# Decode attention over a 4096-key window: one value group's load cut in halves, the output rows ahead of the last values, 360 instead of 320 rows on five DMA engines

## The chip, the core and the metric

One core of a Trainium2 chip. The core has five engines with their own instruction queues: TensorE (PE in the profile, PEld for its weight loads), VectorE (DVE), ScalarE (ACT), GpSimd (POOL) and SyncE (SP), and 16 DMA engines, which carry the transfers that SP and ACT issue. Matmul results go to PSUM, everything else lies in SBUF, on 128 partitions. The metric is the device time of one execution, in microseconds. The kernel before took 194.53 us in the median of 8 runs (194.44 to 195.16).

## The reference, cut to what matters

There is one token, x of 512 elements. Two branches start from its layer norm xn, and the output is `x + s * g`:

```python
q = (xn @ wq) as 32 heads of 128
k, v = the last W = 4096 rows of k_cache, v_cache, per head
scores = q . k * 128 ** -0.5
o = softmax(scores) @ v
s = o (4096 elements) @ wo            # wo: 4096 x 512

g = silu(xn + hs + gelu(layernorm(xn + hs) @ w3) @ w4)    # w3: 512 x 1376, w4: 1376 x 512
```

`hs` is a small shifted product with `w2`. All tensors are bf16. Keys and values of one head are 1 MB each, so 64 MB of the cache are read, beside 4 MB each of `wq` and `wo` and some 3 MB of the other weights.

## The kernel before, in words

The 32 heads are worked on in eight groups of four (`G = 4`). A group's keys are one tile of 128 partitions x 128 rows x 128 elements: each head has 32 partitions, and each partition 128 successive positions, 32 KB in one piece. The values lie the same way. One load is 4 MB.

The loop at the end of the kernel goes over `s = 0 ... 9`. Step `s` scores group `s` and multiplies the values of group `h = s - 2` (`LAG = 2`). The scores of a group are split over two ways: the first 64 or 80 of the 128 rows by VectorE (`k_vector`, L301 and L303), the rest on TensorE (`k_turn`, `k_scores`, with copies on ScalarE, L319). `sm_...` is the softmax. `v_part` (L423) multiplies 128 value tiles into `oT`, one matmul each; `v_out` scales with the reciprocal of the sum (L442 for the last two groups). Three tiles for keys (`K_BUFS`) and two for values (`V_BUFS`) are used in turn, so a load waits until the tile's last reader is done.

All loads but x's are issued by SP, in the order of the code (`load`). Eight semaphores tell of landings and are given to the transfers in turn; a transfer whose semaphore is still in use by an earlier one waits on SP until that one has landed. The order of TensorE, VectorE and ScalarE in the loop is that of the code (`manual_schedule`).

The output product is done in three blocks of heads: 0 to 15 (`y_wide`), 16 to 23 (`y_block(1)`), and 24 to 31, the block `few_block`. For this last one, `wo` lies in two forms. The first `FEW = 320` rows are in `wo_few`, loaded by `load_few`: each of its two transfers has an outermost dimension of `NE = 5`, and each piece of it is four runs of 8 KB; so these rows come by the lowest five DMA engines. To use rows in this layout, `ox_few` spreads the attention output by a matmul with a 0/1 matrix `few` and gives `of`; `y_block(few_block)` multiplies. The rows after that are in `wo_rows`, a head each (`load_rows`, `y_head`): 64 rows of head 26 (`r_part = 64`; `h_part = 26`), then heads 27 to 31. Each output matmul (L150) is four of 128 columns, onto four partitions of `y_ps`.

The end of the kernel, which the change touches: at `s = 7`, SP issues the values of group 5, the rows of block 1 and `load_few`. At `s = 8` it issues the values of group 6 in one load, at `s = 9` the rows of heads 26 and 27, the values of group 7 in three pieces (`cuts = (0, 64, 112, 128)`), and the rows of heads 28 and 29, of 30 and of 31. At `s = 8`, TensorE multiplies block 1 and then group 6's values; VectorE makes `of`. At `s = 9` TensorE takes the first 64 value tiles of group 7, then `wo_few`'s block and the rows of heads 26 and 27, then the other value tiles, then heads 28 to 31. VectorE multiplies the sum with `g` (L602), adds x (L604), and SP stores.

`w4` (1376 rows) is loaded in three transfers, of 8 x 128, 2 x 128 and 96 rows; the columns of `w3` are taken in the order that goes with it (`chunks`).

Of the kernel before, what the change touches and what calls it, by code (L numbers as in the profile page):

```python
# [8 lines left out]
P = 128  # L9
BF16 = mybir.dt.bfloat16  # L10
FP32 = mybir.dt.float32
# [10 lines left out]
NE = 5  # L22
# [7 lines left out]
def kernel(  # L30
# [16 lines left out]
    Bb, Sq, D = A_x.shape  # L47
# [7 lines left out]
    CP = G * W // P  # L55
    PB = P // G
    KC = D // P
    F = B_w3.shape[1]
    assert F == 8 * P + 2 * P + 96
    scale = float(Dh) ** -0.5  # L60


# [3 lines left out]
    const = ctx.enter_context(tc.tile_pool(name="const", bufs=1))  # L66
    small = ctx.enter_context(tc.tile_pool(name="small", bufs=1))
    ps_misc = ctx.enter_context(tc.tile_pool(name="ps_misc", bufs=1, space=PSUM))
# [2 lines left out]
    ps_o = ctx.enter_context(tc.tile_pool(name="ps_o", bufs=1, space=PSUM))  # L71
    ps_y = ctx.enter_context(tc.tile_pool(name="ps_y", bufs=1, space=PSUM))
    sm_pool = ctx.enter_context(tc.tile_pool(name="sm", bufs=3))
    small.tile([P, 112], BF16, name="pad")
    wts_guard = tc.tile_pool(name="wts", bufs=1)
    wts = wts_guard.__enter__()

    def load(dst, src):
        return tc.keep_in_program_order(nc.sync.dma_start(out=dst, in_=src))
# [8 lines left out]
    w3_sb = wts.tile([P, KC, F], BF16, name="w3_sb")  # L88
    load(w3_sb[:], B_w3.rearrange("(p c) n -> p c n", p=P))
    w4_sb = wts.tile([P, 11, D], BF16, name="w4_sb")  # L90
    load(w4_sb[:, 0:8, :], B_w4[0:8 * P, :].rearrange("(p c) n -> p c n", p=P))
    load(w4_sb[:, 8:10, :], B_w4[8 * P:10 * P, :].rearrange("(p c) n -> p c n", p=P))
    load(w4_sb[0:96, 10, :], B_w4[10 * P:F, :])
    wq_sb = wts.tile([P, KC, HD], BF16, name="wq_sb")
    load(wq_sb[:], A_wq.rearrange("(p c) n -> p c n", p=P))
# [1 line left out]
    def load_kv(pool, cache, g, cuts=(0, CP)):  # L97
        t = pool.tile([P, CP, Dh], BF16, tag="kv", name="kv")
        src = cache[0, G * g:G * g + G, W0:, :].rearrange("a (b c) d -> b a (c d)", b=PB)
        dst = t[:].rearrange("p c d -> p (c d)")  # L100
        for c0, c1 in zip(cuts, cuts[1:]):
            load(dst[:, c0 * Dh:c1 * Dh], src[:, :, c0 * Dh:c1 * Dh])
        return t

    ident_bf = const.tile([P, P], BF16, name="ident_bf")
# [95 lines left out]
    nc.vector.tensor_scalar(out=xn_row[:], in0=x_row[:], scalar1=negmean[:], scalar2=rstd[:],  # L201
                            op0=ALU.add, op1=ALU.mult)

    chunks = [(P, slice(r, 8 * P, 8)) for r in range(8)]
    chunks += [(P, slice(8 * P + r, 10 * P, 2)) for r in range(2)]
    chunks += [(96, slice(10 * P, F, 1))]
    a_ps = ps_misc.tile([P, 11], FP32, tag="misc", name="a_ps")
    for j, (m, cols) in enumerate(chunks):
# [45 lines left out]

    few = const.tile([P, 2, 32], BF16, name="few")
    nc.vector.memset(few[:], 0.0)
    for c in range(2):
        nc.vector.tensor_copy(  # L260
            out=few[:, c, 0:4 * NE].rearrange("p (a b) -> p a b", b=4),
            in_=ident_bf[:, 4 * NE * c:4 * NE * (c + 1)].rearrange("p (b a) -> p a b", b=4))

# [112 lines left out]
    blocks = [(0, 16), (16, 8), (24, 8)]  # L378
    few_block = 2
    few_h = blocks[few_block][0]  # L380
    FEW = 8 * 8 * NE
    h_part = few_h + FEW // P

    r_part = FEW % P
    o_blk, wo_blk, ox_blk = {}, {}, {}

    def load_wo(i):
        h0, n = blocks[i]
        load(wo_blk[i], A_wo[h0 * P:(h0 + n) * P, :].rearrange("(p t) n -> p t n", p=P))

    def load_few():
        t = wo_blk[few_block]
        for c in range(2):
            r0 = few_h * P + c * FEW // 2
            load(t[32 * c:32 * c + 4 * NE],
                 A_wo[r0:r0 + FEW // 2, :].rearrange("(b a t) n -> a b (t n)", b=4, a=NE))

    def wo_row(h):
        return wo_rows[:, h - h_part, :]
# [1 line left out]
    def load_rows(h, n):  # L401
        if h == h_part:
            load(wo_rows[r_part:P, 0, :], A_wo[h * P + r_part:(h + 1) * P, :])
            h, n = h + 1, n - 1
        load(wo_rows[:, h - h_part:h - h_part + n, :],
             A_wo[h * P:(h + n) * P, :].rearrange("(h p) n -> p h n", p=P))
# [3 lines left out]
    def v_part(g, v, c0=0, c1=CP):  # L410
        s = st[g]
        if g in MOVED:
            s["ov"] = ps_o.tile([4 * G, 4, Dh], FP32, tag="oT", name="ov")
            for c in range(0, CP, 4):
                nc.tensor.matmul(s["ov"][:], lhsT=s["pT"][:, c:c + 4, :].rearrange("p i a -> p (i a)"),  # L415
                                 rhs=v[:, c:c + 4, :], start=(c == 0), stop=(c == CP - 4))
            s["ov_sb"] = sm_pool.tile([4 * G, 4, Dh], FP32, tag="ov_sb", bufs=1, name="ov_sb")
            nc.scalar.copy(out=s["ov_sb"][:], in_=s["ov"][:])  # L418
            return
        if c0 == 0:  # L420
            s["oT"] = ps_o.tile([P, G], FP32, tag="oT", name="oT")
        for c in range(c0, c1):
            nc.tensor.matmul(s["oT"][:], lhsT=v[:, c, :], rhs=s["pT"][:, c, :], start=(c == 0),  # L423
                             stop=(c == CP - 1))
# [44 lines left out]
        ox_blk[i] = ox  # L469

    def ox_few(i):
        of_ps = ps_misc.tile([64, 8], FP32, tag="misc", name="of_ps")
        nc.tensor.matmul(of_ps[:], lhsT=few[:].rearrange("p a b -> p (a b)"), rhs=ox_blk[i][:],
                         start=True, stop=True)
        of = sm_pool.tile([64, 8], BF16, tag="of", bufs=1, name="of")
        nc.vector.tensor_copy(out=of[:], in_=of_ps[:])
        ox_blk[i] = of

# [22 lines left out]
    NG = H // G  # L501
    cuts = (0, 64, 112, CP)
# [3 lines left out]
    v_pool = None  # L506
    for s in range(NG + LAG):
        h = s - LAG
        last = h == NG - 1
        kn = load_kv(k_pool, A_k_cache, s, (0, 64, CP) if s == 0 else (0, CP)) if s < NG else None  # L510
        if s == LAG:
            wts_guard.__exit__(None, None, None)
            v_pool = ctx.enter_context(tc.tile_pool(name="v", bufs=V_BUFS))
            wo_blk[few_block] = v_pool.tile([64, 8, D], BF16, tag="wo_few", bufs=1, name="wo_few")
            nc.gpsimd.memset(wo_blk[few_block][:], 0.0)
            wo_rows = v_pool.tile([P, H - h_part, D], BF16, tag="wo_rows", bufs=1, name="wo_rows")
            nc.gpsimd.memset(wo_rows[0:r_part, 0, :], 0.0)
        if last:
            load_rows(h_part, 2)
            v = load_kv(v_pool, A_v_cache, h, cuts)  # L520
            for r, n in ((H - G, 2), (H - 2, 1), (H - 1, 1)):
                load_rows(r, n)
        elif h >= 0:
            v = load_kv(v_pool, A_v_cache, h)
        if h == 3:
            wo_24 = k_pool.tile([P, 32, D], BF16, tag="kv", name="wo_24")
            wo_blk[0], wo_blk[1] = wo_24[:, 0:16, :], wo_24[:, 16:24, :]
            load_wo(0)
        if h == 5:
            load_wo(1)  # L530
            load_few()

        if s < NG:
            nb = len(batches(s))

            def keys(b0, b1):
                for b in range(b0, b1):
                    k_turn(s, kn, b)
                    if b > 0:
                        k_scores(s, b - 1)  # L540

            k_open(s)
            k_vector(s, kn, 0)
            keys(0, 2)
            if s > 1:
                sm_den(s - 2)
                sm_rden(s - 2)
            if h - 1 in MOVED:
                v_add(h - 1)
                v_out(h - 1)  # L550
            keys(2, 4)
            k_vector(s, kn, 1)
            if s > 0:
                sm_turn(s - 1)
            if s == 6:
                ox_spread(0)
            keys(4, nb)
            k_scores(s, nb - 1)
            sm_own(s)
            if s > 0:  # L560
                sm_exp(s - 1)
            k_vector(s, kn, 2)
            if s == 6:
                ox_pick(0)
            k_vector(s, kn, 3)
            if h >= 0:
                v_part(h, v)
            sm_max(s)
            if s == 6:
                y_wide(0, 0, 16)  # L570
            if h >= 0 and h not in MOVED:
                v_out(h)
        elif s == NG:

            sm_den(NG - 2)
            sm_rden(NG - 2)
            sm_turn(NG - 1)
            ox_spread(1)
            sm_exp(NG - 1)
            ox_pick(1)  # L580
            y_block(1)
            rows_add(y_ps, one_f, y_row, False)
            v_part(h, v)
            v_out(h)
            ox_spread(few_block)
            sm_den(NG - 1)
            sm_rden(NG - 1)
            ox_pick(few_block)
            ox_few(few_block)
        else:  # L590
            v_part(h, v, 0, cuts[1])
            y_block(few_block)
            for r in range(h_part, H - G):
                y_head(r)
            for c0, c1 in zip(cuts[1:], cuts[2:]):
                v_part(h, v, c0, c1)
            v_out(h)
            for r in range(H - G, H):
                y_head(r)
# [36 lines left out]
```

## Time and profile before

| What | Value |
|---|---|
| median of 8 runs | 194.53 us (194.44 to 195.16) |
| the profiled execution | 194.47 us, of which the span is 192.7 us |
| bytes read from memory | 78.84 MB, 409 GB/s over the span |
| busy, share of the span | PE 69%, PEld 52%, DVE 76%, ACT 44%, POOL 3% |
| the chain that ended last | DVE 51%, DMA 23%, PE 15%, ACT 4%, issue 4% |
| instruction fetches in the span | queue q8: 16 packets, 0.26 MB; q14: 3 packets, 0.02 MB |
| mean granted TensorE clock | 0.696 of full speed |

The span runs from the first to the last instruction. The chain that ended last is followed back from the last instruction, at each step to what released it. "DMA" as a share is the mean busy share of the 16 DMA engines. A line such as L423 is one of the kernel's source, and in a group or a timeline row the columns are the start, the duration, engine, line, operation, `out<-in`, the shapes and the count. Time to landing is from the issue of a transfer to its completion semaphore.

### The profile page before, as it was taken

How to read it: one execution, taken by the hardware profiler on the slowest of the kernel's cores; microseconds unless marked ns; L12 is line 12 of the kernel's file. 1: busy time of each engine (PE TensorE's matmuls, PEld its weight loads, DVE VectorE, ACT ScalarE, POOL GpSimd, SP SyncE). 2: the span in 40 equal slices, each digit the busy share in tenths (PEclk: the TensorE clock that was granted, in tenths of full speed). 3: DMA queues.
4: the chain of work that ended last, by engine and by line, in shares of the span. 5: the costliest groups of instructions: out<-in, count | busy, mean ns of one | idle time of the engine just before them, and what ended most of it. 6: DMA issues, size and time to landing. Idle time of an engine off the chain costs nothing.

```text
span 192.7 us, 4716 instructions
## 1 busy us (share of the span) xinstructions
PE 132.2 (69%) x2098; PEld 99.5 (52%) x2098; DVE 145.8 (76%) x160; ACT 85.6 (44%) x193; POOL 6.5 (3%) x14
## 2 busy tenths in 40 slices
PE   0549774967625579878586994981888878843882
PEld 0444364756524433467475343881768256832771
DVE  1550207999999999999999999996899999950201
ACT  2003003888895270458357413771475069841000
POOL 2110007000000000000000000000000000000000
PEclk9999955596975556985558699555555599855555
DMA  6999999999999999999999999999999999999980
GB/s 203 412 488 422 398 429 459 417 435 412 422 432 435 435 437 432 435 435 429 432 432 435 435 432 401 469 432 415 435 432 437 418 435 393 447 416 393 423 332 15
DMA packets 4869, 79.13 MB, mean 411 GB/s; under 512 B 682, under 2 KB 1482, under 8 KB 1866
## 3 DMA queue, kind: packets, MB, share of 16 engines
q1 hardware_dynamic: 4698, 78.84, 96.1%
q8 instruction: 16, 0.26, 0.6%
q10 hardware_dynamic: 152, 0.00, 0.0%
q14 instruction: 3, 0.02, 0.0%
HBM read 78.84 MB, written 0.00 MB: 409 GB/s over the span
## 4 chain that ended last, share of the span: by engine, by line
DVE 51%; DMA 23%; PE 15%; ACT 4%; issue 4%; POOL 1%; SPq 0%; ACTq 0%; POOLq 0%
DVE S L303 30%; DVE prod L301 16%; DMA kv<-in_A_k_cache_dram 13%; DMA kv<-in_A_v_cache_dram 9%; ACT kt L319 3%; PE yr_ps L489 3%; PE oT L423 3%; PE hr_ps L221 2%; DMA x_bf<-in_A_x_dram 2%; PE qT_ps L237 2%; PE a_ps L210 1%; PE hr_ps L218 1%; DVE S L339 1%; DVE m L341 1%; PE sT L325 1%
## 5 line engine op out<-in xcount | busy, mean ns | idle before, releaser
L303 DVE TENSOR_REDUCE S<-prod 128x20 f32<-128x2560 bf16 (+1 forms) x32 | 83.8, 2620 | 1.1
L319 ACT COPY kt<-pt 128x1024 bf16<-128x1024 bf16 x54 | 52.9, 1014 | 23.9 <-PE pt L317 23.2
L317 PE MATMUL pt<-ident_bf,kv 128*128 128x128 bf16 x432 | 43.7, 267 | 10.0 <-DMA kv<-in_A_k_cache_dram 7.2
L301 DVE TENSOR_TENSOR prod<-kv,q_bc 128x2560 bf16<-128x2560 bf16 (+1 forms) x32 | 44.3, 1386 | 5.3 <-DMA kv<-in_A_k_cache_dram 2.5
L317 PEld LDWEIGHTS <-kv 128*128 128x128 bf16 x432 | 35.1, 122 | 12.4 <-DMA kv<-in_A_k_cache_dram 7.5
L325 PE MATMUL sT<-qT_bf,kt 128*128 128x4 bf16 x432 | 20.0, 168 | 17.3 <-ACT kt L319 16.5
L325 PEld LDWEIGHTS <-kt 128*128 128x128 bf16 x432 | 16.6, 104 | 24.7 <-ACT kt L319 24.5
L423 PE MATMUL oT<-pT,kv 128*128 128x4 bf16 x768 | 21.5, 166 | 3.5 <-DMA kv<-in_A_v_cache_dram 3.4
L423 PEld LDWEIGHTS <-kv 128*128 128x128 bf16 x768 | 21.0, 103 | 5.3 <-DMA kv<-in_A_v_cache_dram 5.2
L415 PE MATMUL ov<-kv,pT 128*16 128x512 bf16 x64 | 18.6, 463 | 0.0
L363 ACT ACTIVATE pT<-S,mb 128x128 bf16<-128x128 f32 x32 | 13.9, 569 | 0.3
L415 PEld LDWEIGHTS <-pT 128*16 128x16 bf16 x64 | 6.5, 105 | 11.1 <-issue 6.4
L442 DVE TENSOR_TENSOR o<-oT,rden 128x4 bf16<-128x4 f32 x2 | 0.3, 162 | 13.5 <-PE oT L423 13.5
L334 ACT ACTIVATE own<-sT,par 128x48 f32<-128x48 f32 (+1 forms) x32 | 7.6, 359 | 3.7 <-PE sT L325 3.7
L363 ACT ACTIVATION_READ_ACCUMULATOR pT<-S,mb 128x1 f32 x32 | 8.1, 254 | 0.0
L446 ACT ACTIVATE o<-oT,rden 128x1 bf16<-128x1 f32 x24 | 4.3, 260 | 8.5 <-PE oT L430 5.0
L418 ACT COPY ov_sb<-ov 16x512 f32<-16x512 f32 x2 | 1.2, 576 | 14.6 <-PE ov L415 14.6
L224 DVE COPY hr<-hr_ps 1x512 f32<-1x512 f32 x1 | 0.7, 679 | 8.9 <-PE hr_ps L221 8.9
L347 PE MATMUL mt_ps<-ident_f,m 128*1 128x128 f32 x8 | 2.9, 359 | 5.0 <-DVE rden L374 5.0
L489 PE MATMUL yr_ps<-wo,ox 128*1 128x512 bf16 x16 | 5.4, 513 | 0.9 <-DVE ox L467 0.9
L213 ACT ACTIVATE a_bf<-a_ps 128x10 bf16<-128x10 f32 x1 | 0.2, 180 | 12.0 <-PE a_ps L210 12.0
L356 PE MATMUL mb_ps<-md,par_t 5*128 5x4 f32 x16 | 3.9, 314 | 2.3 <-DVE md L351 1.5
(113 smaller groups left out, 90.8 us busy)
## 6 DMA issues: line engine op xcount, KB each, us to landing
kv<-in_A_k_cache_dram SPq DMA_DIRECT2D x7, 4096.0 KB, 31.1
kv<-in_A_v_cache_dram SPq DMA_DIRECT2D x7, 4096.0 KB, 30.5
wq_sb<-in_A_wq_dram SPq DMA_DIRECT2D x1, 4096.0 KB, 17.8
kv<-in_A_k_cache_dram SPq DMA_DIRECT2D x2, 2048.0 KB, 21.3
wo<-in_A_wo_dram SPq DMA_DIRECT2D x1, 2048.0 KB, 30.1
kv<-in_A_v_cache_dram SPq DMA_DIRECT2D x1, 2048.0 KB, 13.8
kv<-in_A_v_cache_dram SPq DMA_DIRECT2D x1, 1536.0 KB, 16.8
w_sb<-in_B_w_dram SPq DMA_DIRECT2D x1, 1376.0 KB, 6.8
```

The source lines that it names most:

```text
L301: nc.vector.tensor_tensor(out=prod[:, 0:m, :], in0=kn[:, rows, :], in1=q_bc[:, g:g + 1, :].to_broadcast([P, m, Dh]), op=ALU.mult)
L303: nc.vector.tensor_reduce(out=st[g]["S"][:, rows], in_=prod[:, 0:m, :], axis=AX.X, op=ALU.add)
L317: nc.tensor.transpose(pt[:, c - c0, :], kn[:, c, :], ident_bf[:])
L319: nc.scalar.copy(out=kts[b][:, 0:c1 - c0, :], in_=pt[:, 0:c1 - c0, :])
L325: nc.tensor.matmul(st[g]["sT"][:, c - nd(g), :], lhsT=kt[:, c - c0, :], rhs=qT_bf[:, G * g:G * g + G], start=True, stop=True)
L334: nc.scalar.mul(s["own"][:, 0:m, a], s["sT"][:, 0:m, a], par[:, a:a + 1])
L356: nc.tensor.matmul(mb_ps[:], lhsT=par_t[:].rearrange("k b a -> k (b a)"), rhs=md[:], start=True, stop=True)
L363: nc.scalar.activation(out=s["pT"][:, :, a], in_=s["S"][:], func=ACT.Exp, scale=scale, bias=mb[:, a:a + 1], accum_out=s["sum"][:, a:a + 1])
L415: nc.tensor.matmul(s["ov"][:], lhsT=s["pT"][:, c:c + 4, :].rearrange("p i a -> p (i a)"), rhs=v[:, c:c + 4, :], start=(c == 0), stop=(c == ...
L423: nc.tensor.matmul(s["oT"][:], lhsT=v[:, c, :], rhs=s["pT"][:, c, :], start=(c == 0), stop=(c == CP - 1))
L446: nc.scalar.mul(o_blk[b][:, c + k:c + k + 1], st[g]["oT"][:, k:k + 1], st[g]["rden"][:, k:k + 1])
L489: nc.tensor.matmul(yr[i][:], lhsT=ox_blk[i][:, t:t + 1], rhs=wo_blk[i][:, t, :], start=(t == 0), stop=(t == n - 1))
```

## The change

- The values of group 6, the last but one, are loaded in two halves of 64 rows, each with its own semaphore.
- At `s = 9`, TensorE does `wo_few`'s block and heads 26 and 27 first, and then all value tiles of group 7.
- `FEW` is 360 instead of 320: `wo_few` is loaded in three transfers of 5 x 3 runs of 8 KB, and 24 instead of 64 rows of head 26 are left for `wo_rows`. The 0/1 matrix and its result become 96 wide.
- `w4`'s first 1280 rows come in one load instead of two, with ten rows per partition, and the columns of `w3` follow it.
- A pad of 112 elements becomes one of 80.

```diff
-    small.tile([P, 112], BF16, name="pad")
+    small.tile([P, 80], BF16, name="pad")
...
-    load(w4_sb[:, 0:8, :], B_w4[0:8 * P, :].rearrange("(p c) n -> p c n", p=P))
-    load(w4_sb[:, 8:10, :], B_w4[8 * P:10 * P, :].rearrange("(p c) n -> p c n", p=P))
+    load(w4_sb[:, 0:10, :], B_w4[0:10 * P, :].rearrange("(p c) n -> p c n", p=P))
...
-    chunks = [(P, slice(r, 8 * P, 8)) for r in range(8)]
-    chunks += [(P, slice(8 * P + r, 10 * P, 2)) for r in range(2)]
+    chunks = [(P, slice(r, 10 * P, 10)) for r in range(10)]
...
-    few = const.tile([P, 2, 32], BF16, name="few")
+    few = const.tile([P, 3, 32], BF16, name="few")
     nc.vector.memset(few[:], 0.0)
-    for c in range(2):
+    for c in range(3):
         nc.vector.tensor_copy(
-            out=few[:, c, 0:4 * NE].rearrange("p (a b) -> p a b", b=4),
-            in_=ident_bf[:, 4 * NE * c:4 * NE * (c + 1)].rearrange("p (b a) -> p a b", b=4))
+            out=few[:, c, 0:3 * NE].rearrange("p (a b) -> p a b", b=3),
+            in_=ident_bf[:, 3 * NE * c:3 * NE * (c + 1)].rearrange("p (b a) -> p a b", b=3))
...
-    FEW = 8 * 8 * NE
+    FEW = 9 * 8 * NE
...
-        for c in range(2):
-            r0 = few_h * P + c * FEW // 2
-            load(t[32 * c:32 * c + 4 * NE],
-                 A_wo[r0:r0 + FEW // 2, :].rearrange("(b a t) n -> a b (t n)", b=4, a=NE))
+        for c in range(3):
+            r0 = few_h * P + c * FEW // 3
+            load(t[32 * c:32 * c + 3 * NE],
+                 A_wo[r0:r0 + FEW // 3, :].rearrange("(b a t) n -> a b (t n)", b=3, a=NE))
...
-        of_ps = ps_misc.tile([64, 8], FP32, tag="misc", name="of_ps")
+        of_ps = ps_misc.tile([96, 8], FP32, tag="misc", name="of_ps")
...
-        of = sm_pool.tile([64, 8], BF16, tag="of", bufs=1, name="of")
+        of = sm_pool.tile([96, 8], BF16, tag="of", bufs=1, name="of")
...
-            wo_blk[few_block] = v_pool.tile([64, 8, D], BF16, tag="wo_few", bufs=1, name="wo_few")
+            wo_blk[few_block] = v_pool.tile([96, 8, D], BF16, tag="wo_few", bufs=1, name="wo_few")
...
-            v = load_kv(v_pool, A_v_cache, h)
+            v = load_kv(v_pool, A_v_cache, h, (0, 64, CP) if h == NG - 2 else (0, CP))
...
         else:
-            v_part(h, v, 0, cuts[1])
             y_block(few_block)
             for r in range(h_part, H - G):
                 y_head(r)
-            for c0, c1 in zip(cuts[1:], cuts[2:]):
+            for c0, c1 in zip(cuts, cuts[1:]):
                 v_part(h, v, c0, c1)
```

More of the change, by code (lines that the diff above doesn't have):

```diff
@@ L58 @@
     F = B_w3.shape[1]
-    assert F == 8 * P + 2 * P + 96
+    assert F == 10 * P + 96
     scale = float(Dh) ** -0.5
```

## The prediction

> **What bounds the kernel now.** I read the DMA part of the page first, then the chain that ended last, the TensorE timeline of the end, and the DMA share over the last microseconds.
>
> The row of DMA busy tenths over 40 slices, and the queues:
>
> ```profile
> DMA  6999999999999999999999999999999999999980
> q1 hardware_dynamic: 4698, 78.84, 96.1%
> q8 instruction: 16, 0.26, 0.6%
> q14 instruction: 3, 0.02, 0.0%
> ```
>
> The 16 DMA engines are full from the second slice to the last but one: the span is the time of 78.84 MB. VectorE's large shares of the chain lie in the middle, where it runs beside full DMA engines. So the end is looked at, first in the chain of waits (start, us, what):
>
> ```profile
> 169.65 16.80 DMA kv<-in_A_v_cache_dram
> ...
> 186.50 1.88 PE oT L423 x64
> ...
> 188.62 0.71 PE y_ps L150 x16
> ```
>
> and in the TensorE timeline (start, us, instructions, in brackets the idle time before and who ended it):
>
> ```profile
> 177.52 3.57 PE L423 MATMUL oT<-pT,kv 128*128 128x4 bf16 x128 [2.92 <-DMA kv<-in_A_v_cache_dram]
> ...
> 182.86 1.87 PE L423 MATMUL oT<-pT,kv 128*128 128x4 bf16 x64
> 184.66 1.02 PE L150 MATMUL y_ps<-wo_few,of 64*1 64x128 bf16 x32
> 185.61 0.38 PE L150 MATMUL y_ps<-wo_rows,o 128*1 128x128 bf16 x8
> 186.50 1.87 PE L423 MATMUL oT<-pT,kv 128*128 128x4 bf16 x64 [0.51 <-DMA kv<-in_A_v_cache_dram]
> ```
>
> TensorE waits for a transfer at 177.5 (all of group 6's values) and at 186.5 (the second piece of group 7's). The last transfer of all, the rows of head 31, was issued at 177.5; the tile view of `wo_rows`, cut to that issue, gives its time to landing:
>
> ```profile
> DMA to landing us min/median/max: 11.5/11.5/11.5
> ```
>
> It lands at 189.0, and the last four matmuls start at 189.03, after a short gap: values and last rows end together, and both are transfers. Last, the windows (length, then busy time of each engine, granted clock, DMA share, GB/s):
>
> ```profile
> 182.00:185.00 3.00, 2.31 (x82) 2.19 (x85) 0.65 (x3) 0.00 (x0) 0.00 (x0) 0.50 0.97 398
> 185.00:187.00 2.00, 1.49 (x54) 0.99 (x43) 0.00 (x0) 0.00 (x0) 0.00 (x0) 0.50 0.83 322
> 187.00:189.00 2.00, 1.75 (x64) 1.58 (x62) 0.16 (x1) 0.00 (x0) 0.00 (x0) 0.50 0.39 138
> ```
>
> The share falls over 4 us: the engines end unevenly, and the slowest ends the kernel. Which one that is, the packet records tell. They hold start, duration, size and queue of each packet; an engine starts a packet some 4 ns before its previous one ends, so the packets join into 16 chains, and the five that carry 8 KB packets of `wo_few` are the five low engines. My joining (us from the span's start; v5 is value group 5, and so on):
>
> ```
> engines            v5 ends        few ends   v6 ends        v7 piece 2     last packet
> A, B, C            160.8-161.0    165.7-.9   175.4-175.5    184.6-184.8    187.2-187.4
> D                  161.8          166.7      176.5          185.6          188.3
> E                  162.2          167.1      176.95         186.04         188.67
> three without few  160.9-161.2    -          173.0-173.4    182.3-182.7    184.9-185.3
> eight without few  162.4-164.3    -          174.7-176.6    184.1-185.8    186.7-188.4
> ```
>
> E, one of the five, is last at every mark. It is late because it fetched 8 KB of instructions twice (at 70.0 and 147.0): eight 32 KB packets take an engine 9.68 us, 10.36 with such a fetch, 11.2 with one of 16 KB, of which the lower eight rows of the table have two each.
>
> **The change part by part.**
>
> *360 rows.* Each of the five engines carried 2 x 4 packets of 8 KB, now 3 x 3. A packet takes 309 ns, less 4 of overlap, and each transfer ends in a 9 ns semaphore packet: +0.305 + 0.009 = +0.314 us. The rows left of head 26 fall from 64 (four 1 KB packets per engine) to 24. A 1 KB packet takes 46 ns, 42 net. How 24 rows are split no row shows: between two per engine and all on one (24 x 0.042 = 1.0 us, +0.84 over now, if that one is E). 64 rows spread evenly on 16 and 20 pieces evenly on five, so I take two each: -0.084 on E. [...]
>
> *Group 6 in halves.* Sixteen 16 KB packets for eight of 32 KB: 16 x (611 - 4) = 9712 ns against 8 x (1213 - 4) = 9672, and one more semaphore: +0.045. The semaphore packet is 9 ns within a stream that is full. [...]
>
> *w4 in one load.* Eight packets of 8 KB and eight of 2 KB (84 ns) become eight of 10 KB, estimated at 385 ns, halfway between 309 (8 KB) and 460 (12 KB): 3048 against 3080 ns, and a semaphore less: -0.037.
>
> *TensorE's order.* Half of group 6's 128 matmuls can run before 177.5: its first half should land near 172.6 (half of 9.7 us earlier), and TensorE is free from 174.6. So oT ends some 1.7 us earlier, near 179.5, the chain to `of` (181.1 to 183.0 now) near 181.3, and the 32 + 8 output matmuls (1.02 + 0.38) fill the wait before the first piece of group 7, which lands at 182.8. Its 64 matmuls then end near 184.9 where TensorE was done at 186.0. None of it shortens the path: the next thing is the second piece, at 186.45, and TensorE already had 0.51 us of idle time there. A gain is excluded while that transfer is last; a loss starts only if the new order is over 1.9 us late (186.7 - 184.8).
>
> *Issues and waits.* SP issues one load fewer at the start, one more of few (0.83 us) and one more for group 6 (0.58), all far ahead: group 6's values are issued at 149.4 and reached at 163.4 at the earliest. Eight completion semaphores are taken in turn, so the shift of one changes what SP waits for: the 24 rows now wait for keys 7, head 27's rows for values 5, the last two rows for the halves of group 6. Behind them on SP stands group 7's first piece, issued at 169.05 when TensorE has freed its buffer; values 5 must have landed before that matmul (165.6), so nothing is later. If it landed after 169.05, group 7 would be. The last rows' issue still follows group 6's landing (177.5), 7 us before any engine reaches it.
>
> *Small tiles.* `few` has a third 128x15 copy on VectorE in the prologue, POOL fills 96 partitions where it filled 64 (3.5 us at 30.0, the load at 132): covered by full DMA queues, and by the 13 us between the issue of keys 6 at 111.5 and 124.4, when the queue reaches them. The pad moves addresses only.
>
> The sum on E: 0.314 - 0.084 + 0.045 - 0.037 = +0.24 us, for both its second piece (186.04) and its last packet (188.67), hence for the end. The next engine's last packet (188.37) gets no few rows and doesn't overtake. The profiled execution took 194.47 us (span 192.7 and 1.8 around it), 0.06 under the median 194.53. Its end moves to 194.71; against the median, 194.77.
>
> **The rivals.**
>
> *The five engines are relieved (faster).* E's lateness is two fetches of 0.68 us and D's is one (about 1.0). If the changed program's fetches fall on other engines, D and E end near 187.6, and the others set the end at 188.37 - 0.08: 0.4 us earlier, 194.1. For it: the placing depends on the program. Against: instruction counts are almost equal, and the same engine was hit twice.
>
> *One more fetch on a late engine (slower).* It decides as soon as one more 8 KB fetch falls on E, or a 16 KB one on any that ends after 187.4: 0.24 + 0.68 = 0.92, 195.45; with 24 rows on one engine, 0.24 + 0.92 = 1.16, 195.7. For it: the same kernel without change ran from 194.44 to 195.16, so such differences occur. Against: five of eight runs lie within 0.1 us.
>
> *TensorE's order was what bound (faster).* Then 1.1 us of its 1.7 would show, 193.4. Against: the wait of 0.51 us at 186.5 is named as a transfer, and the last rows land at 189.0 whatever TensorE does.
>
> *The halves do nothing,* the matmuls wait for both: the time is the likeliest case's, 194.77, since that part has no price on the path.
>
> **How the numbers follow.** 0.2% is 0.39 us, about what a measurement can tell from no change. Likeliest, +0.24 (own range +0.1 to +0.38, from the packet prices and another placing of the 24 rows), with the halves' rival in it: 0.50, within 0.2%. One more fetch or a bad placing: 0.32, slower. Fetches elsewhere 0.15 and TensorE's order 0.03: faster. The range leaves out the 0.03 and the worst tenth above: 194.05 to 195.6.
>
> **What would show it.** Right: TensorE waits longer than 0.51 us ahead of the second piece of group 7, which lands near 186.7; group 6's matmuls in two runs of 64, the second from 177.7; head 31's rows land near 189.2; 8 KB packets nine on each of five chains. Wrong: the second piece landing before 186.3 or after 187.0, the last rows landing clearly apart from it, or no wait of TensorE at the end.

## The result, and the profile after

The changed kernel took 197.99 us in the median of 11 runs (197.08 to 199.5), beside 194.74 us for the kernel before in 32 runs (194.44 to 196.4): a ratio of 1.0163, 95% interval 1.0138 to 1.0188, some 3.2 us slower. The forecast was 194.77 us with a range up to 195.6. The profiled execution took 198.02 us, its span is 196.2 us.

The rows of the page that answer to those shown of before, DMA busy tenths and GB/s over 40 slices (4.9 us each), and the queues, for the changed kernel:

```profile
DMA  5999999999999999999999999999999999999980
GB/s 199 421 489 427 391 424 463 421 427 424 427 424 427 434 439 434 441 434 438 421 431 434 424 414 438 444 424 441 417 436 424 427 429 307 297 430 400 381 313 11
...
q1 hardware_dynamic: 4664, 78.84, 96.0%
q8 instruction: 16, 0.26, 0.5%
q14 instruction: 3, 0.02, 0.0%
```

The bytes, the instruction fetches and the busy share are those of before. But two slices near 162 to 172 us move 307 and 297 GB/s where their neighbours move 429 and 430. The DMA engines are as busy as ever there, and slower. The windows over that place (length, then busy time of PE, PEld, DVE, ACT, POOL, granted clock, DMA share, GB/s), first of the kernel before:

```profile
163.00:166.00 3.00, 2.19 (x51) 1.90 (x52) 2.96 (x2) 2.55 (x6) 0.00 (x0) 1.00 1.06 448
166.00:169.00 3.00, 3.00 (x118) 3.00 (x115) 2.93 (x3) 2.10 (x11) 0.00 (x0) 0.77 1.05 448
169.00:172.00 3.00, 1.37 (x6) 1.02 (x6) 1.87 (x7) 0.72 (x4) 0.00 (x0) 0.50 1.05 448
```

and of the changed kernel:

```profile
163.00:166.00 3.00, 2.18 (x39) 1.78 (x37) 2.97 (x2) 2.25 (x5) 0.00 (x0) 0.86 1.01 295
166.00:169.00 3.00, 3.00 (x118) 3.00 (x118) 2.93 (x3) 2.46 (x13) 0.00 (x0) 0.71 1.07 279
169.00:172.00 3.00, 1.78 (x22) 1.45 (x19) 1.86 (x7) 0.72 (x5) 0.00 (x0) 0.50 0.94 341
```

Over these 9 us the share stays near 1, and the rate falls from 448 to 279 to 341 GB/s. The packet records give 4.01 MB before and 2.73 MB after for packets that start there; 1.28 MB at 411 to 448 GB/s is 2.9 to 3.1 us. That is the loss, but for some tenths. It falls where the engines reach `wo_few`: in the chains of the prediction they did so after 160.8 to 162.2.

What it does to the end, in the chain of waits of the changed kernel (start, us, what), its TensorE timeline, the landing of head 31's rows in the tile view of `wo_rows`, and the last windows:

```profile
170.12 19.95 DMA kv<-in_A_v_cache_dram
190.12 1.88 PE oT L421 x64
...
192.24 0.69 PE y_ps L149 x16
```

```profile
175.34 1.87 PE L421 MATMUL oT<-pT,kv 128*128 128x4 bf16 x64 [0.51 <-DMA kv<-in_A_v_cache_dram]
180.45 1.87 PE L421 MATMUL oT<-pT,kv 128*128 128x4 bf16 x64 [3.25 <-DMA kv<-in_A_v_cache_dram]
...
184.27 1.02 PE L149 MATMUL y_ps<-wo_few,of 96*1 96x128 bf16 x32 [0.25 <-DVE of L474]
185.08 0.43 PE L149 MATMUL y_ps<-wo_rows,o 128*1 128x128 bf16 x8
186.26 1.87 PE L421 MATMUL oT<-pT,kv 128*128 128x4 bf16 x64 [0.75 <-DMA kv<-in_A_v_cache_dram]
190.12 1.87 PE L421 MATMUL oT<-pT,kv 128*128 128x4 bf16 x64 [1.98 <-DMA kv<-in_A_v_cache_dram]
```

```profile
DMA to landing us min/median/max: 12.2/12.2/12.2
```

```profile
182.00:185.00 3.00, 1.86 (x48) 1.57 (x49) 1.22 (x6) 0.00 (x0) 0.00 (x0) 0.50 1.00 374
185.00:187.00 2.00, 1.25 (x47) 0.96 (x37) 0.00 (x0) 0.00 (x0) 0.00 (x0) 0.50 0.98 369
187.00:189.00 2.00, 1.13 (x43) 1.05 (x39) 0.00 (x0) 0.00 (x0) 0.00 (x0) 0.50 0.85 326
```

The end has the form that was forecast: group 6 in two runs of 64 matmuls, the output matmuls ahead of group 7, TensorE waiting for the second piece. But this piece came at 190.07 where 186.7 was forecast, and head 31's rows, issued at 180.4 when group 6's second half had landed, at 192.6, where 189.2 was. The DMA share from 187 to 189 is 0.85 where it was 0.39. What is carried after 172 us is late by some 3 to 4 us.

### The profile page after: what moved, and what is told of

It is laid out like the page before. It is cut to its first block, busy times and chain, and to the rows that moved or that the text cites. A ratio compares the mean times of both kernels' runs of the same rounds, so it can differ in the third digit from the quotient of the medians.

```text
span 196.2 us, 4718 instructions
## 1 busy us (share of the span) xinstructions
PE 135.8 (69%) x2098; PEld 103.2 (53%) x2098; DVE 145.9 (74%) x161; ACT 86.1 (44%) x193; POOL 6.5 (3%) x14
## 4 chain that ended last, share of the span: by engine, by line
DVE 42%; DMA 39%; PE 11%; ACT 5%; issue 1%; SPq 0%; ACTq 0%
DMA kv<-in_A_k_cache_dram 27%; DVE S L301 25%; DVE prod L299 13%; DMA kv<-in_A_v_cache_dram 10%; ACT kt L317 4%; PE pt L315 3%; PE oT L421 3%; PE yr_ps L487 3%; DMA x_bf<-in_A_x_dram 2%; PE sT L323 2%; DVE S L337 1%; DVE m L339 1%; DVE mx L347 1%; ACT own L332 0%; DVE md L349 0%
## 5 line engine op out<-in xcount | busy, mean ns | idle before, releaser
L315 PE MATMUL pt<-ident_bf,kv 128*128 128x128 bf16 x432 | 47.4, 282 | 10.3 <-DMA kv<-in_A_k_cache_dram 8.5
L315 PEld LDWEIGHTS <-kv 128*128 128x128 bf16 x432 | 38.0, 129 | 12.7 <-DMA kv<-in_A_k_cache_dram 9.3
L421 PEld LDWEIGHTS <-kv 128*128 128x128 bf16 x768 | 21.1, 104 | 7.8 <-DMA kv<-in_A_v_cache_dram 7.7
L354 PEld LDWEIGHTS mb_ps<-md,par_t 5*128 5x128 f32 x16 | 3.6, 276 | 3.1 <-PE sT L323 2.1
```

The source lines that it names most:

```text
L315: nc.tensor.transpose(pt[:, c - c0, :], kn[:, c, :], ident_bf[:])
L354: nc.tensor.matmul(mb_ps[:], lhsT=par_t[:].rearrange("k b a -> k (b a)"), rhs=md[:], start=True, stop=True)
```

## The experiments

The theories, by the letters that the expectations use. H: the halves cost the time; R: the 360 rows do; B: only both together. D: the destination partitions of `wo_few` do, some of which the 360-row layout changes. The packet records hold neither a destination nor an engine's number: the destinations are read from the code, where each transfer of `wo_few` has five outermost parts, and that each engine carries one part is taken from the five chains, each with eight of the 40 packets of 8 KB; engine `a` is the one with part `a`. That the five, or the eight of `e11_eight`, are the lowest of the 16 no record shows. "An engine's own group" is, here and in the expectations, the four partitions that its part has in the layout of before, and no other tie between an engine and a partition is meant. S: it is the third transfer, or the source, or 360 rows as such. F and G: TensorE runs out of fetched instructions, by the new order alone (F) or only with the halves (G); the last three expectations use F for either. W: `w4` in one load. All runs of one batch share the runs of the kernel before, and each ratio is to these: 194.74 us in the first batch and in the last, 195.16 and 194.76 in the two between. Single runs of the unchanged kernel spread over 1% (194.46 to 196.42 in the last batch), so a single time says little, and a ratio is taken over the runs of both kernels; it is not the quotient of the two medians.

### One part at a time

Halves alone, on the kernel before (`e1_halves`):

```diff
-            v = load_kv(v_pool, A_v_cache, h)
+            v = load_kv(v_pool, A_v_cache, h, (0, 64, CP) if h == NG - 2 else (0, CP))
```

> The kernel before with one edit: group 6's values in two halves. Theory H (the 16 KB pieces of the halves make the transfers slow between 163 and 172 us of the changed kernel): nearly the whole loss comes with this edit alone, 197 to 198 us, and the rate between 163 and 172 is near 300 GB/s as in the changed kernel. Theory R (the 360 rows in three transfers do it): 194.5 to 194.7, and 440 GB/s there, as before. Theory B (only both together): 194.5 to 194.7 as well.

The 360 rows alone, on the kernel before (`e2_rows360`): `FEW`, `few`, `load_few` and the 96-wide tiles as in the change, nothing else.

> The kernel before with 360 rows in three transfers instead of 320 in two, nothing else. Theory R: 197 to 198 us and near 300 GB/s between 163 and 172. Theory H: 194.7 to 194.9, the 0.23 us that the prediction gave to this part, and 440 GB/s there. Theory B: the same 194.7 to 194.9.

The changed kernel with group 6 in one load (`e3_after_whole`):

```diff
-            v = load_kv(v_pool, A_v_cache, h, (0, 64, CP) if h == NG - 2 else (0, CP))
+            v = load_kv(v_pool, A_v_cache, h)
```

> The changed kernel with group 6's values in one load again. Theory H: 194.6 to 195.0, no dip between 163 and 172. Theory R: still 197 to 198. Theory B: 194.6 to 195.0.

The changed kernel with 320 rows in two transfers as before (`e4_after_320`):

```diff
-    FEW = 9 * 8 * NE
+    FEW = 8 * 8 * NE
...
-        for c in range(3):
-            r0 = few_h * P + c * FEW // 3
-            load(t[32 * c:32 * c + 3 * NE],
-                 A_wo[r0:r0 + FEW // 3, :].rearrange("(b a t) n -> a b (t n)", b=3, a=NE))
+        for c in range(2):
+            r0 = few_h * P + c * FEW // 2
+            load(t[32 * c:32 * c + 4 * NE],
+                 A_wo[r0:r0 + FEW // 2, :].rearrange("(b a t) n -> a b (t n)", b=4, a=NE))
```

> The changed kernel with 320 rows in two transfers again, and the halves, TensorE's order and w4 as changed. Theory H: still 197 to 198 and the dip between 163 and 172. Theory R and theory B: 194.4 to 194.7 and no dip.

| Kernel | median, us | ratio, 95% interval |
|---|---|---|
| halves alone | 194.73 | 0.9996 (0.9975 to 1.0018) |
| 360 rows alone | 198.16 | 1.019 (1.0161 to 1.0218) |
| changed, group 6 in one load | 198.05 | 1.0174 (1.0149 to 1.0199) |
| changed, 320 rows | 196.04 | 1.0069 (1.0052 to 1.0085) |

The 360 rows alone give the whole loss, and without the halves nothing comes back. The halves by themselves cost nothing that can be measured. But the fourth run does not return to 194.74: there is a second loss of 1.3 us, which the changed kernel hides. It is taken up below.

### Which thing about the 360 rows

In the layout of before, part `a` of the five goes to partitions `32c + 4a` to `32c + 4a + 3`. In the layout of the change it goes to `32c + 3a` to `32c + 3a + 2`: in the first two transfers, part 0 stays within the first group of four, and parts 3 and 4 lie wholly in a lower neighbour's. The third transfer goes to partitions 64 to 78, where none of the five has a group. Together 33 of the 45 pieces, 264 of 360 KB, lie outside the engine's own groups. Two runs on the kernel before keep its two transfers and 320 rows and move only the destination, by two partitions (`e5_shift2`: half of each engine's rows in the next group) and by four (`e6_shift4`: all of them); `few` follows. For D, two partitions higher are a dip to some 300 GB/s between 163 and 169 us and 196.5 to 198.5 us; if only a group that two parts share costs, four higher are free, 194.4 to 194.9.

```diff
-            load(t[32 * c:32 * c + 4 * NE],
+            load(t[32 * c + 2:32 * c + 2 + 4 * NE],
```

> The kernel before with one edit: the 320 rows go to partitions two higher, so that each of the five engines writes partitions 4a+2 to 4a+5 and no longer 4a to 4a+3; the rows and bytes read, the packets and the engines are the same. [...] Theory S (the source addresses, the third transfer or its length do it): 194.4 to 194.9, no dip.

> The same with four partitions instead of two: each engine writes a whole group of four, but the next engine's. [...] Theory D with any group that isn't the engine's own: 196.5 to 198.5 and the dip. Theory S: 194.4 to 194.9.

A third puts the 320 rows 64 partitions higher (`e12_upper`), at partitions 64 to 83 and 96 to 115, with tiles of 128 and a smaller pad. If any place but the own groups costs, that is 197 to 199 us and the dip:

```diff
-            load(t[32 * c:32 * c + 4 * NE],
+            load(t[64 + 32 * c:64 + 32 * c + 4 * NE],
```

> The kernel before with the 320 rows in partitions 64 to 83 and 96 to 115 instead of 0 to 19 and 32 to 51, whole groups of four per engine still. [...] If only the five engines among themselves collide (as with two or four partitions higher): 194.4 to 195.0 and no dip.

The counter-test keeps 360 rows and three transfers, and gives each engine its own groups (`e7_rows360_aligned`): the first 320 as before, the other 40 rows, one piece per engine, to partitions 0, 4, 8, 12 and 16 of a free part of the tile of the other output rows. The product leaves these 40 rows out.

```diff
...
+        load(wo_24[0:4 * NE:4, 24:32, :],
+             A_wo[few_h * P + FEW:few_h * P + ROWS, :].rearrange("(a t) n -> a t n", a=NE))
```

> The kernel before with 360 rows on the five engines, but the first 320 laid as before (four partitions of its own per engine and transfer) and the other 40 by a third transfer, one 8 KB piece per engine to partition 4a of a free part of the tile of the other output rows; head 26 keeps 24 rows. The product leaves out those 40 rows, so the output is not the reference's. Theory D: 194.6 to 195.0, the +0.24 us of the prediction, with no dip. Theory S: 196.5 to 198.5 and the dip.

| Kernel | median, us | ratio, 95% interval |
|---|---|---|
| two partitions higher | 196.73 | 1.0069 (1.0039 to 1.0099) |
| four partitions higher | 198.36 | 1.0155 (1.0118 to 1.0191) |
| 64 partitions higher | 198.19 | 1.0171 (1.0136 to 1.0206) |
| 360 rows, own groups | 194.88 | 0.9983 (0.9951 to 1.0015) |

The windows of the same stretch, four partitions higher:

```profile
163.00:166.00 3.00, 2.31 (x48) 1.79 (x46) 2.93 (x5) 2.95 (x4) 0.00 (x0) 1.00 1.02 295
166.00:169.00 3.00, 2.44 (x72) 2.31 (x70) 2.93 (x3) 2.50 (x11) 0.00 (x0) 0.67 1.18 336
```

64 partitions higher:

```profile
163.00:166.00 3.00, 2.10 (x47) 1.67 (x44) 2.94 (x3) 2.60 (x3) 0.00 (x0) 0.95 1.19 292
166.00:169.00 3.00, 3.00 (x98) 2.97 (x95) 2.93 (x3) 2.74 (x13) 0.00 (x0) 0.50 1.04 235
```

360 rows in their own groups:

```profile
163.00:166.00 3.00, 2.10 (x45) 1.67 (x46) 2.93 (x4) 2.77 (x3) 0.00 (x0) 1.00 1.02 429
166.00:169.00 3.00, 3.00 (x98) 2.96 (x97) 2.93 (x3) 2.69 (x13) 0.00 (x0) 0.54 1.16 500
169.00:172.00 3.00, 2.00 (x49) 1.62 (x45) 2.47 (x7) 0.76 (x6) 0.00 (x0) 0.50 0.89 377
```

Over these 9 us the last kernel moves 435 GB/s, the kernel before 448 and the changed one 305. The dip comes and goes with the destination, with 320 rows as with 360, with two transfers as with three. S falls, D stands. The packets show how far it reaches. Median ns of those that start between 163 and 170 us, by size; the 8 KB ones are `wo` rows, the 32 KB ones values:

```
kernel                     8 KB    32 KB
before                     309     1213
360 rows alone             440     1842
two partitions higher      344     1486
four partitions higher     428     1812
64 partitions higher       616     2222
360 rows, own groups       309     1213
```

The values are carried by all 16 engines and go, by the code, to the same 128 partitions in every kernel, and they are slowed too. Joined into chains as in the prediction, an engine that carries no `wo_few` row takes 9.68 us for its eight 32 KB packets of group 6 before (163.34 to 173.02), and 12.04 us with the 360 rows (163.43 to 175.47). So the price is not paid on the five engines alone. In the changed kernel itself the 8 KB packets take 476 ns, and the 16 KB packets of group 6's halves 971 ns, where they take 611 with the halves alone.

Of these layouts, only the one in the own groups is free of cost (0.9983, the others 1.0069 to 1.019). What slows the packets in the others no run shows, nor why the engines that carry no `wo_few` row slow down with them (9.68 to 12.04 us).

### The destinations put right in the changed kernel, and the second loss

The order of TensorE alone (`e8_order`) and the order with the halves (`e9_halves_order`), both on the kernel before:

```diff
-            v_part(h, v, 0, cuts[1])
...
-            for c0, c1 in zip(cuts[1:], cuts[2:]):
+            for c0, c1 in zip(cuts, cuts[1:]):
```

> The kernel before with TensorE's new order at the end alone: the output rows ahead of all of group 7's value tiles. Theory F (the 1.3 us of the changed kernel with 320 rows come from TensorE running out of fetched instructions, and the order does that alone): 195.5 to 196.2, with waits for issue of over 1 us in TensorE's last 20 us. Theory G (the order does it only with the halves, which take the waits away that hid the fetches): 194.5 to 195.0 and no such wait.

> The kernel before with group 6 in halves and TensorE's new order, and neither the 360 rows nor w4's edit. Theory G (the two together take away the waits in which TensorE's instruction fetches were hidden): 195.7 to 196.4, with TensorE waiting for issue for more than 1 us twice after 175 us, the second time within the last value tiles. Theory W (w4's edit has a part in it): 194.5 to 195.0 and no such wait in the last value tiles.

Then the whole change with 320 of its 360 rows in the engines' own groups (`e13_after_aligned`): two transfers of four pieces per engine as before, and a third of one piece to partition `64 + 4a`; and the same with group 6 in one load (`e14_aligned_whole`). The third transfer's 40 KB still lie outside the own groups, in the upper 64 partitions, where the 320 rows of `e12_upper` cost 1.0171:

```diff
...
+        n = 4 * 8 * NE
+        for c in range(2):
+            r0 = few_h * P + c * n
+            load(t[32 * c:32 * c + 4 * NE],
+                 A_wo[r0:r0 + n, :].rearrange("(b a t) n -> a b (t n)", b=4, a=NE))
+        load(t[64:64 + 4 * NE:4],
+             A_wo[few_h * P + 2 * n:few_h * P + FEW, :].rearrange("(a t) n -> a t n", a=NE))
```

> The changed kernel complete, but with its 360 rows written in the order of before: two transfers of four pieces per DMA engine to partitions 4a to 4a+3, and a third of one piece per engine to partition 64+4a; the matrix few follows. D with F (each engine's own group of four partitions is free of cost, and the halves with the new order make TensorE run out of instructions): 196.0 to 196.4, no dip of the rate between 163 and 170 us, and idle times of TensorE put down to issue, near 1.4 us in group 6's second half and near 2.4 us in group 7's values, as with 320 rows (196.04). D without F (the 1.3 us of that run came from its two transfers): 194.5 to 195.1. S (the third transfer, or 360 rows as such, is what costs): 197.8 to 198.3 with the dip.

> As the one before, but group 6's values in one load; all else of the change is in. D with F: 194.4 to 194.9, no dip, no idle time put down to issue at the end. F wrong (the order alone costs 1.3 us): 195.9 to 196.4. S: 197.8 to 198.3.

And the order with group 6 cut at 96 of its 128 tiles (`e15_cut96`), which leaves TensorE's instructions as they are with the cut at 64:

```diff
-            v = load_kv(v_pool, A_v_cache, h)
+            v = load_kv(v_pool, A_v_cache, h, (0, 96, CP) if h == NG - 2 else (0, CP))
```

> The kernel before with group 6's load cut at 96 instead of 64 of its 128 tiles, and with the new order of TensorE. The instructions of TensorE are the same as with the cut at 64. F (TensorE runs out of instructions at a place of the program): the stop is again ahead of group 6's 103rd tile, so six tiles into the second part, and again ahead of group 7's 58th; 196.0 to 196.5 against 196.33 with the cut at 64. Rival L (the stop hangs on the landing of the second part: 38 tiles after it): the second part has 32 tiles, so no first stop, and 194.5 to 195.0.

| Kernel | median, us | ratio, 95% interval |
|---|---|---|
| order alone | 194.7 | 0.9999 (0.9965 to 1.0032) |
| halves and order | 196.33 | 1.0064 (1.0038 to 1.0091) |
| changed, 320 rows in own groups | 196.56 | 1.008 (1.0048 to 1.0112) |
| the same, group 6 in one load | 195.03 | 1.0 (0.9973 to 1.0028) |
| order, cut at 96 | 196.67 | 1.0098 (1.0061 to 1.0134) |

Putting these destinations right, with all else of the change in place, takes the kernel from 197.99 to 196.56, and one load for group 6 takes it to 195.03. So the losses don't add: the second shows only where the first is gone. The three medians 196.56, 195.03 and 196.67 lie 0.13 to 0.17 us above what was expected. In the second the misplaced 40 KB can be seen: an engine that carries no `wo_few` row takes 10.03 us for its eight packets of group 6 (163.28 to 173.31), where it takes 9.68 before and with 360 rows in own groups (163.33 to 173.01). TensorE's timeline of the changed kernel with 320 rows in own groups:

```profile
178.27 1.17 PE L425 MATMUL oT<-pT,kv 128*128 128x4 bf16 x38 [0.97 <-DMA kv<-in_A_v_cache_dram]
180.36 0.86 PE L425 MATMUL oT<-pT,kv 128*128 128x4 bf16 x26 [0.92 <-issue]
...
184.34 1.68 PE L425 MATMUL oT<-pT,kv 128*128 128x4 bf16 x57
188.67 2.05 PE L425 MATMUL oT<-pT,kv 128*128 128x4 bf16 x71 [2.65 <-issue]
190.97 0.60 PE L149 MATMUL y_ps<-wo_rows,o 128*1 128x128 bf16 x16 [0.25 <-DVE o L444]
```

with group 6 in one load besides:

```profile
178.06 3.57 PE L425 MATMUL oT<-pT,kv 128*128 128x4 bf16 x128 [3.39 <-DMA kv<-in_A_v_cache_dram]
...
184.75 1.87 PE L425 MATMUL oT<-pT,kv 128*128 128x4 bf16 x64
186.94 1.86 PE L425 MATMUL oT<-pT,kv 128*128 128x4 bf16 x64 [0.32 <-DMA kv<-in_A_v_cache_dram]
189.06 0.67 PE L149 MATMUL y_ps<-wo_rows,o 128*1 128x128 bf16 x16 [0.25 <-DVE o L444]
```

and with the cut at 96 on the kernel before:

```profile
174.90 3.02 PE L423 MATMUL oT<-pT,kv 128*128 128x4 bf16 x102
180.06 0.86 PE L423 MATMUL oT<-pT,kv 128*128 128x4 bf16 x26 [2.14 <-issue]
...
184.12 1.68 PE L423 MATMUL oT<-pT,kv 128*128 128x4 bf16 x57
188.25 2.04 PE L423 MATMUL oT<-pT,kv 128*128 128x4 bf16 x71 [2.45 <-issue]
```

TensorE stops in the middle of a run of matmuls whose data have landed, and the stop is put down to nothing that the profile shows ("issue"). It comes after tile 64 + 38 = 102 of group 6 and after tile 57 of group 7; with the cut at 96 it is after tile 102 again. So it belongs to a place in the program, not to a transfer: L falls. In three of the kernels with such a stop (changed with 320 rows in own groups, changed with 320 rows in all, cut at 96), a 16 KB packet of the instruction queue ends 1.3 to 1.5 us before each of the two stops ends (178.90, 178.89 and 178.67 against 180.36, 180.25 and 180.06; 187.26, 187.10 and 186.95 against 188.67, 188.44 and 188.25). Over all 17 kernels here, the 103rd tile of group 6 never starts earlier than 1.36 us after the end of the 16 KB packet that comes between 177.7 and 179.6: with a stop 1.36 to 1.48 us after it, without one 1.65 us or more. TensorE waiting for instructions that come late is what this speaks for; no run moved a fetch by itself.

The halves alone have the first stop too, before group 6's 103rd tile, and a short one before the 34th of the 40 output matmuls that follow group 7's first piece:

```profile
180.43 0.85 PE L423 MATMUL oT<-pT,kv 128*128 128x4 bf16 x26 [1.64 <-issue]
...
185.68 0.27 PE L150 MATMUL y_ps<-wo_rows,o 128*1 128x128 bf16 x1
186.60 0.38 PE L150 MATMUL y_ps<-wo_rows,o 128*1 128x128 bf16 x7 [0.66 <-issue]
186.91 1.86 PE L423 MATMUL oT<-pT,kv 128*128 128x4 bf16 x64
```

From the 103rd tile to this place there are 127 matmuls, as there are to group 7's 58th tile in the new order, so the two stops are the same distance apart in the program. The time is not longer for it (0.9996): the last 64 tiles start at 186.91, where the kernel before starts them at 186.50 when their data land. With the new order the second stop lies in group 7's tiles, and pushes the last 71 of them past the landing of everything. G stands in that the loss comes only with both, and F as the order alone falls. But G's reason, that the halves take waits away, covers the first stop only. At the second, TensorE is hardly earlier than without the halves: with the halves and the order it is done with 57 tiles at 186.06, and with group 6 in one load (`e14_aligned_whole`) it starts the 58th at 186.29. It is the packet that is later, 187.19 against 184.80. Why it is later with the two together stayed open. In the changed kernel TensorE waits for the late transfers (0.51, 3.25, 0.75 and 1.98 us above) and has no such stop.

### The small edit, and a try at a faster kernel

`w4` in one load, on the kernel before (`e10_w4`), as in the change's diff.

> The kernel before with w4's first 1280 rows in one load and the columns of w3 to match, nothing else. Both theories: the time of the kernel before within 0.3 us (the prediction gave it -0.04). Were it 195.5 or more, the 1.3 us would be w4's.

194.55 us, ratio 0.998 (0.9956 to 1.0004): nothing that can be measured, as forecast (-0.04). The halves and the order lose without this edit, so W falls.

Since the prediction's joining showed three engines without few rows idle early (last packets at 184.9 to 185.3), `e11_eight` gives 512 rows to eight engines, in the same layout of four partitions a part, `32c + 4a` to `32c + 4a + 3`, and drops the rows of heads 26 and 27:

```diff
-NE = 5
+NE = 8
...
```

> The kernel before with 512 rows (heads 24 to 27 whole) on the lowest eight DMA engines instead of 320 on five, in two transfers, four partitions of its own per engine and transfer; the rows of heads 26 and 27 need no load of their own. The eight keep the 64 KB that five of them had, three that ended some 3 us early get it too, and all 16 lose the 12 KB per engine of those rows, 12 packets of 1 KB at 42 ns: 0.5 us. Theory D (only a group of partitions that isn't the engine's own slows): no dip, and 193.9 to 194.4, under the kernel before. If the slowing grows with the number of engines on this load instead: 196 or more, and a dip between 163 and 169.

A miss: 195.75 us, ratio 1.004 (1.0016 to 1.0064). The rate has no dip (451 and 459 GB/s from 163 to 169). In its profiled execution (196.40 us) two of the eight engines end their last packets at 190.36 and 190.47 and the other fourteen between 184.9 and 188.7. Both reach the end of group 5's values at 164.6 and 164.7, where the other six of the eight are there at 161.5 to 162.9, and each had one 16 KB instruction fetch after 60 us; what else put them behind was not followed further.

No kernel here is faster than the one before beyond what can be measured.

## Why the prediction was wrong

**What bounds the kernel.** Right, and still so: 16 full DMA engines, and the second piece of group 7 on the path.

**360 rows, +0.314 us on five engines.** This step failed, by a factor of ten. It took the 8 KB packet at 309 ns from a trace in which the packets of `wo_few`, as the runs show, went where they cost nothing more, and read `3 x 3` pieces as only one piece more. The diff also changed `4 * NE` to `3 * NE` in the destination and added a third block of partitions, and the prediction passed over both, though the diff shows them. By the runs, the price is the rate of all 16 engines, which falls from 448 to 279 to 341 GB/s over 163 to 172 us: 3.4 us alone (1.019). With every row in its engine's own groups, the terms of the sum can't be told from nothing: 0.9983 on the kernel before (interval 0.9951 to 1.0015), where the sum says +0.23. With 40 KB still misplaced and the rest of the change but the halves, it is 195.03 against 194.74 us (interval of the ratio 0.9973 to 1.0028), where the sum says +0.19.

**Bounds from both sides.** The prediction bounded the 24 rows (-0.084 to +0.84) and left the 360 rows without an upper bound, because the trace seemed to show their price. It showed it for another layout. The 24 rows were not timed by themselves; where the joined packets can be told apart, most engines carry two of them and a few none; the prediction took two on E.

**Halves, +0.045.** Not contradicted for the transfers: 0.9996 alone (0.9975 to 1.0018), which is -0.49 to +0.35 us of 194.74, so one more transfer shows no cost beyond that. **`w4`, -0.037.** Not contradicted (0.9956 to 1.0004).

**TensorE's order, 0, "a loss starts only if the new order is over 1.9 us late".** Right alone (0.9999). With the halves it fails, by something that was not thought of: TensorE stops twice with its data in place, most likely for its next instructions. The stops make it over 1.9 us late, and 1.3 to 1.9 us come out (196.04 to 196.67). The changed kernel doesn't show it: its data are later still, and its time is that of the 360 rows alone (197.99 against 198.16).

**Issues and waits, 0.** Nothing speaks against it: SP issued group 7's first piece at 169.51, and the engines, then slow, reached it no earlier than before.

**The rivals.** The slower one had the sign and not the mechanism: the fetches are the same 16 and 3 packets, and its worst case, 195.7, is far below. The halves do let TensorE start earlier (two runs of 64), without a gain. That the order was what bound is refuted by the run with it alone.

**The signs.** "The second piece after 187.0" was named as a sign of error, and it came at 190.07. The wait ahead of it is longer than 0.51 us, as foretold (1.98), which shows how little a sign is worth that any late transfer gives.

## What to carry to other kernels

A transfer over a few partitions has two sizes and a place: see from the code which part of it goes to which partitions, keep each part on those for which the rate was measured, or measure anew (four partitions higher cost 1.0155 here), and look at GB/s beside the DMA share, since full engines can be slow ones (279 GB/s at a share of 1.07). A packet's price is that of the layout it was measured in (8 KB: 309 ns, and 428 four partitions higher). When waits for data are taken away from a long run of matmuls, look for "issue" in the middle of a run, and for a packet of the instruction queue that ends shortly before (1.3 to 1.5 us before the end of the stop here). Two losses on parallel paths can hide one another, as the 1.3 us of TensorE's stops were hidden here; take each out alone and both together.

## What was not expected of the hardware

Writing the same 320 KB (five engines, 64 KB each) four or 64 partitions higher lowered the rate of all 16 from 448 to 235 to 336 GB/s over 163 to 169 us and cost 1.0155 to 1.0171. With half of it outside the own groups the ratio was 1.0069, and with 264 of the 360 KB 1.019, whose interval (1.0161 to 1.0218) overlaps those of the 320 KB. So the half cost less than the whole; whether the loss goes by the bytes alone, and by what means, stayed open. TensorE stopped for up to 2.65 us in a run of matmuls with its data in place, at the same instructions with group 6 cut at 64 and at 96, and each of these stops ended 1.3 to 1.5 us after a packet of the instruction queue.
